# Attention and MLP-mixer on one core: the weighted sum P·V in plain float32, two heads side by side on TensorE

## The chip, the cores and the metric

One Trainium2 chip, one of its cores. The metric is the device time of one execution in microseconds (us). The kernel before took 702.86 us, the median of 3 runs (702.39 to 704.26).

## The reference

q, k and v are [4, 8, 576, 64] in float32: batch, heads, positions, head size. All matrix products are asked for in float32, and the output is float32.

```python
q_rot, k_rot = (rotate(q), rotate(k))            # rotary positions, halves of 32
scores = scale * np.matmul(q_rot, k_rot.transpose(0, 1, 3, 2))
scores = scores - np.max(scores, axis=-1, keepdims=True)
attn = np.exp(scores)
attn = attn / (np.sum(attn, axis=-1, keepdims=True) + 1e-09)
x = np.matmul(attn, v)                           # then heads side by side: [4, 576, 512]
h = np.maximum(x.transpose(0, 2, 1) @ w_tok1, 0.0) @ w_tok2        # [576, 256], [256, 576]
u = x + h.transpose(0, 2, 1)
out = u + np.maximum(u @ w_ch1, 0.0) @ w_ch2     # [512, 1536], [1536, 512]
```

The weights of the mixer come as 64-bit floats and are split on the chip.

## The kernel before

**Two stages.** `attention` (L205) works through 16 pairs of heads, `mixers` (L669) through the token and the channel products. Between them stands the splitting of the token weights (`tok_weights`, L642), which is queued into the first pairs of attention: each block of 512 columns is taken apart by `f64_split` (L579) in some ten instructions on ACT, DVE and POOL.

**Two-part numbers.** TensorE multiplies `float32r`, a float32 cut to fewer bits, in one pass. So every factor is kept as a high part (ACT writes it, rounded) and a low part (DVE subtracts the high part from the original), and a product is made of several float32r matmuls.

**A pair.** 576 positions are four blocks of 128 and a tail of 64. A pair of heads has nine tiles of scores: four blocks for each head, and one tile that holds both heads' tails (`TILES`, L394). For each tile: the scores on TensorE (`qk`, L426 and L435, 4 or 6 matmuls of 288 columns), the negated row maximum on DVE (`mx`, L440), the exponential with its row sum on ACT (`ex`, L450), four transpositions of P on TensorE (`tr`, L460), a copy of the high part by ACT (`eh`, L465) and the subtraction that makes the low part by DVE (`el`, L469). The last 64 columns of P go in groups of two or three tiles through `tt_` (L490), `th` (L496) and `tl` (L499).

**The weighted sum.** The transposed P of a head is collected in two chunks of 256 or 320 query columns. A chunk takes nine matmuls (`pv`, L514). The stationary operand is V with its high part in columns 0 to 63 and its low part in columns 64 to 127 (made by POOL, L272 and L275), so one matmul multiplies with both; four row blocks go once with the high part of P, four with its low part, and in the ninth both parts of the tail stand above each other. The sums for V's two parts come out on the two halves of the partitions, so ACT copies one half (`p1`, L517) and DVE adds the other (`p2`, L520) into `oT`. Then `oT` is transposed back (L547, L550), copied to X (L556) and divided by the row sums (L566, L559).

**The order.** No loop sets it. `Plan` (L56) is a list scheduler: each piece is a task with an engine, an estimated duration, what it depends on, the buffers that it holds and a priority; a piece with alternatives goes to the engine that would end it first. Priorities in attention are the pair's and tile's number plus an offset per kind of piece, the table `AT` (L143). `SLACK` (L145) says how much later than the earliest possible piece a piece may start and still be taken for its priority. Scores have two PSUM buffers (`s`), everything else of TensorE's results shares four (`t`).

Of the kernel before, what the change touches and what calls it, by code (L numbers as in the profile page):

```python
# [55 lines left out]
class Plan:  # L56


    def __init__(self):
        self.tasks = []  # L60
        self.clock = {e: 0.0 for e in LAG}

# [25 lines left out]
    def run(self):  # L88
# [10 lines left out]
        while left:  # L99
# [13 lines left out]
            for eng, lst in best.items():  # L113
                first = min(x[0] for x in lst)
                x = min((x for x in lst if x[0] <= first + SLACK[eng]), key=lambda x: (x[1], x[0]))
                if pick is None or x[0] < pick[0]:
                    pick = x
# [34 lines left out]
def dve(n):  # L152
    return n / 960 + 0.07
# [15 lines left out]
def rope_attention_mixer_kernel(ctx: ExitStack, tc: tile.TileContext, q, k, v, w_tok1, w_tok2, w_ch1, w_ch2, tab, out):  # L169
# [8 lines left out]
    nc = tc.nc  # L178
# [26 lines left out]
    def attention(ctx):  # L205
# [3 lines left out]
        def slots(nm, n, shape, dt=F32, pool=pers, fifo=True):  # L209
# [4 lines left out]
               "v": slots("vraw", 1, [P, 2, R + 1, D])}  # L214
# [32 lines left out]
        def prep(n):  # L247
# [4 lines left out]
            for nm, src, pr in (("k", k, 0.0), ("q", q, 0.5), ("v", v, 1.0)):  # L252
# [12 lines left out]
                if nm == "v":  # L265
                    l.append(add("SP", 0.65, ldt(TL), bufs=[rb], prio=pos + AT["load"] + pr))
                n5 = 2 * (R + 1) * D
                if nm == "v":
                    vb = Buf(vss)

                    def v1(e, rb=rb, vb=vb):
                        return lambda: e.tensor_copy(out=vb.t[:, :, :, 0:D], in_=rb.t.rearrange("p h r d -> p r h d"))  # L272

                    def v2(e, rb=rb, vb=vb):
                        return lambda: e.tensor_tensor(out=vb.t[:, :, :, D:2 * D], in0=rb.t.rearrange("p h r d -> p r h d"),  # L275
                                                       in1=vb.t[:, :, :, 0:D], op=ALU.subtract)
# [117 lines left out]
        TILES = [(0, 0), (0, 1), (0, 2), (0, 3), None, (1, 2), (1, 3), (1, 0), (1, 1)]  # L394
        CHUNK = [(0, 1), (2, 3, 4), (4, 5, 6), (7, 8)]
        W2 = S // 2

        def pair(n):
            b, hp = divmod(n, HP)
            lb = Buf(ls)  # L400
            pt = [Buf(pts) for _ in CHUNK]
            pb, tr_done, exps, el_of = {}, {}, {}, {}
# [5 lines left out]
            chunk_ev = {c: [] for c in range(4)}  # L408

            def dests(t):  # L410
                if t == 4:
                    return [(1, 0, TL, 2 * P), (2, TL, TL, 2 * P)]
                c = {0: 0, 1: 0, 2: 1, 3: 1, 5: 2, 6: 2, 7: 3, 8: 3}[t]
                return [(c, 0, P, TILES[t][1] % 2 * P)]

            oT = Buf(oTs)
            pv_done = []
            for t in range(9):
                g = 9 * n + t
                sb = Buf(s_ps)  # L420
                if TILES[t] is None:
# [6 lines left out]
                else:  # L428
                    h, j = TILES[t]
# [15 lines left out]
                def ex(sb=sb, nm=nm, p=pb[t], t=t):  # L445
                    if TILES[t] is None:
                        l = lb.t[:, R, 0:1]
                    else:
                        l = lb.t[:, TILES[t][1], TILES[t][0]:TILES[t][0] + 1]
# [3 lines left out]
                x = add("ACT", 0.73, ex, [x], [sb, nm, pb[t], lb], g + AT["ex"])  # L453
                exps[t] = x
                tb = Buf(t_ps)
                new = [pt[c] for c, s0, w, d0 in dests(t)]
# [5 lines left out]
                x = add("PE", 0.45, tr, [x], [tb, pb[t]] + new, g + AT["tr"])  # L462
                for c, s0, w, d0 in dests(t):
                    def eh(tb=tb, c=c, s0=s0, w=w, d0=d0):
                        nc.scalar.copy(out=pt[c].t[:, 0:R, d0:d0 + w],  # L465
                                       in_=tb.t.rearrange("p (j q) -> p j q", j=R)[:, :, s0:s0 + w])

                    def el(tb=tb, c=c, s0=s0, w=w, d0=d0):
# [7 lines left out]
                end = {1: 0, 4: 1, 6: 2, 8: 3}.get(t)  # L476
                if end is None:
                    continue

                ts = {0: (0, 1), 1: (2, 3, 4), 2: (5, 6), 3: (7, 8)}[end]  # L480
                tb = Buf(t_ps)
                ev = {}
                for x, tt in enumerate(ts):
                    for c, s0, w, d0 in dests(tt):
                        a = ev.setdefault(c, [x * P + s0, d0, 0])
                        a[2] += w

                def tt_(tb=tb, ts=ts):
                    for x, tt in enumerate(ts):
                        nc.tensor.transpose(tb.t[0:TL, x * P:(x + 1) * P], pb[tt].t[:, M:S], ident)  # L490

                x = add("PE", 0.11 * len(ts), tt_, [exps[tt] for tt in ts],
                        [tb] + [pb[tt] for tt in ts] + [pt[c] for c in ev], g + AT["tt"])
                for c, (s0, d0, w) in ev.items():
                    def th(tb=tb, c=c, s0=s0, w=w, d0=d0):
                        nc.scalar.copy(out=pt[c].t[0:TL, R, d0:d0 + w], in_=tb.t[0:TL, s0:s0 + w])  # L496

                    def tl(tb=tb, c=c, s0=s0, w=w, d0=d0):
                        nc.vector.tensor_tensor(out=pt[c].t[TL:P, R, d0:d0 + w], in0=tb.t[0:TL, s0:s0 + w],  # L499
                                                in1=pt[c].t[0:TL, R, d0:d0 + w], op=ALU.subtract)  # L500
                    x3 = add("ACT", act(w), th, [x], [tb, pt[c]], g + AT["th"])
                    x4 = add("DVE", dve(w), tl, [x3], [tb, pt[c]], g + AT["tl"])
                    chunk_ev[c] += [x3, x4]
# [419 lines left out]
```

## Time and profile before

The profiled execution spans 700.2 us from its first to its last instruction. The median of the runs, 702.86 us, is 2.7 us above that; this much lies around the span.

| engine | busy us | share of the span |
|---|---|---|
| PE (TensorE matmul) | 655.4 | 94% |
| PEld (its weight loads) | 589.1 | 84% |
| DVE | 513.6 | 73% |
| ACT | 378.0 | 54% |
| POOL | 332.9 | 48% |

How to read it: the shares are averages over two unlike stages. The attention stage lasts until about 328 us, the mixers from there to the end. A matmul's busy time contains its way through the array, so busy time of PE overstates what it has to do; the distance from one matmul's start to the next one's start is the better measure.

### The profile page before, as it was taken

How to read it: one execution, taken by the hardware profiler on the slowest of the kernel's cores; microseconds unless marked ns; L12 is line 12 of the kernel's file. 1: busy time of each engine (PE TensorE's matmuls, PEld its weight loads, DVE VectorE, ACT ScalarE, POOL GpSimd, SP SyncE). 2: the span in 40 equal slices, each digit the busy share in tenths (PEclk: the TensorE clock that was granted, in tenths of full speed). 3: DMA queues.
4: the chain of work that ended last, by engine and by line, in shares of the span. 5: the costliest groups of instructions: out<-in, count | busy, mean ns of one | idle time of the engine just before them, and what ended most of it. 6: DMA issues, size and time to landing. Idle time of an engine off the chain costs nothing.

```text
span 700.2 us, 11545 instructions
## 1 busy us (share of the span) xinstructions
PE 655.4 (94%) x3960; PEld 589.1 (84%) x3960; DVE 513.6 (73%) x937; ACT 378.0 (54%) x917; POOL 332.9 (48%) x348
## 2 busy tenths in 40 slices
PE   1778989999999999996999999999999999999997
PEld 1667878899999999995787998998989989899895
DVE  5999999999999999997785789736943583233322
ACT  3678888899999999996443444422421321111010
POOL 3989997887777777602650546502700250000000
PEclk9999999999999999999899999999999999999999
DMA  7466545465655555450110123201300100001112
GB/s 204 128 171 164 139 117 146 103 155 148 147 148 145 148 146 148 113 149 0 54 60 1 46 76 105 76 1 61 90 31 0 62 1 1 0 1 46 75 61 90
DMA packets 45433, 62.28 MB, mean 89 GB/s; under 512 B 13888, under 2 KB 26944, under 8 KB 45376
## 3 DMA queue, kind: packets, MB, share of 16 engines
q1 hardware_dynamic: 44832, 60.91, 32.3%
q8 instruction: 31, 0.51, 0.3%
q10 hardware_dynamic: 544, 0.66, 0.3%
q14 instruction: 26, 0.21, 0.1%
HBM read 30.41 MB, written 4.72 MB: 50 GB/s over the span
## 4 chain that ended last, share of the span: by engine, by line
PE 60%; DVE 27%; ACT 6%; issue 4%; DMA 2%; POOL 0%; DVEq 0%; SPq 0%; ACTq 0%; POOLq 0%
PE m L801 21%; PE m L824 21%; DVE nm L440 9%; DVE pt L469 8%; PE m L718 4%; PE m L740 4%; PE t L514 3%; DVE oT L520 2%; ACT p L450 2%; DVE pt L499 2%; ACT pt L465 1%; PE s L435 1%; DVE ql L335 1%; PE m L779 1%; PE t L460 1%
## 5 line engine op out<-in xcount | busy, mean ns | idle before, releaser
L803 ACT ACTIVATE gh<-m 128x384 fp32r<-128x384 f32 x72 | 35.5, 493 | 190.8 <-PE m L801 174.6
L450 ACT ACTIVATE p<-s,nm 128x576 f32<-128x576 f32 x144 | 107.9, 750 | 17.0 <-DVE nm L440 14.6
L440 DVE TENSOR_REDUCE nm<-s 128x1 f32<-128x576 f32 x144 | 107.3, 746 | 1.6 <-PE s L435 0.8
L469 DVE TENSOR_TENSOR pt<-t,pt 128x512 fp32r<-128x512 f32 (+1 forms) x160 | 97.6, 628 | 3.0 <-ACT pt L465 1.7
L801 PE MATMUL m<-uh,c1h 128*128 128x384 f32 x288 | 97.0, 337 | 0.0
L801 PE MATMUL m<-uh,c1l 128*128 128x384 f32 x288 | 96.6, 336 | 0.0
L801 PE MATMUL m<-ul,c1h 128*128 128x384 f32 x288 | 96.6, 335 | 0.0
L514 PE MATMUL t<-pt,vs 128*128 128x256 f32 (+1 forms) x576 | 92.3, 304 | 4.1 <-DVE pt L469 2.0
L805 DVE SCALAR_TENSOR_TENSOR gl<-m,gh 128x384 fp32r<-128x384 f32 x72 | 39.6, 555 | 70.5 <-ACT gh L803 70.3
L435 PE MATMUL s<-khd,qs 128*128 128x288 f32 x256 | 81.9, 336 | 8.1 <-ACT p L450 7.2
L460 PE MATMUL t<-ident,p 128*128 128x128 f32 x576 | 85.0, 275 | 4.4 <-DVE pt L499 2.7
L514 PEld LDWEIGHTS t<-pt,vs 128*128 128x128 f32 x576 | 78.8, 188 | 10.5 <-DVE pt L469 3.9
L826 DVE TENSOR_TENSOR X<-m,X 128x512 f32<-128x512 f32 x64 | 44.2, 690 | 58.6 <-PE m L824 58.6
L465 ACT CAST pt<-t 128x512 fp32r<-128x512 f32 (+1 forms) x160 | 84.1, 550 | 5.3 <-PE t L460 4.4
L824 PE MATMUL m<-c2h,gl 128*128 128x512 f32 x216 | 85.1, 394 | 0.0
L824 PE MATMUL m<-c2l,gh 128*128 128x512 f32 x216 | 85.0, 393 | 0.0
L824 PE MATMUL m<-c2h,gh 128*128 128x512 f32 x216 | 84.8, 393 | 0.0
L460 PEld LDWEIGHTS t<-ident,p 128*128 128x128 f32 x576 | 67.5, 141 | 7.6 <-DVE pt L499 3.4
L435 PE MATMUL s<-kld,qs 128*128 128x288 f32 x256 | 72.5, 299 | 0.0
L435 PEld LDWEIGHTS s<-khd,qs 128*128 128x128 f32 x256 | 49.2, 192 | 16.2 <-ACT p L450 13.2
L611 POOL TENSOR_TENSOR fa<-fc,fa 128x384 f32<-128x384 f32 (+2 forms) x24 | 28.7, 1199 | 57.2 <-DVE fa L609 57.2
L801 PEld LDWEIGHTS m<-uh,c1h 128*128 128x128 f32 x288 | 54.1, 188 | 0.9
(126 smaller groups left out, 1355.6 us busy)
## 6 DMA issues: line engine op xcount, KB each, us to landing
khd<-kh SPq DMA_DIRECT2D x62, 144.0 KB, 2.5
kld<-kl SPq DMA_DIRECT2D x62, 144.0 KB, 2.7
stg<-in_moe_w_ch_dram SPq DMA_DIRECT2D x16, 384.0 KB, 3.2
stg<-in_moe_w_ch_dram SPq DMA_DIRECT2D x12, 512.0 KB, 3.6
kraw<-in_k_dram SPq DMA_DIRECT2D x16, 256.0 KB, 3.0
qraw<-in_q_dram SPq DMA_DIRECT2D x16, 256.0 KB, 3.1
vraw<-in_v_dram SPq DMA_DIRECT2D x16, 256.0 KB, 2.9
out_dram<-X SPq DMA_DIRECT2D x16, 256.0 KB, 2.1
```

The source lines that it names most:

```text
L435: nc.tensor.matmul(sb.t[:, c, 0:W2], a, m.t[:, h, c * W2:(c + 1) * W2], start=(x == 0), stop=(x == 1))
L440: nc.vector.tensor_reduce(out=nm.t, in_=sb.t[:, :, 0:W2], axis=AX.XY, op=ALU.max, negate=True)
L450: nc.scalar.activation(out=p.t.rearrange("p (a b) -> p a b", a=2), in_=sb.t[:, :, 0:W2], func=ACTF.Exp, bias=nm.t, accum_out=l)
L460: nc.tensor.transpose(tb.t[:, j * P:(j + 1) * P], p.t[:, j * P:(j + 1) * P], ident)
L465: nc.scalar.copy(out=pt[c].t[:, 0:R, d0:d0 + w], in_=tb.t.rearrange("p (j q) -> p j q", j=R)[:, :, s0:s0 + w])
L469: nc.vector.tensor_tensor(out=pt[c].t[:, R + 1:2 * R + 1, d0:d0 + w], in0=tb.t.rearrange("p (j q) -> p j q", j=R)[:, :, s0:s0 + w], in1=pt ...
L514: nc.tensor.matmul(ab.t[:, 0:w], vb.t[:, r, h], pt[c].t[:, j, 0:w], start=(x == 0), stop=(x == 2 * R))
L801: nc.tensor.matmul(tb.t[:, 0:N], a, m, start=(i == 0), stop=(i == len(lst) - 1))
L803: x = add("ACT", 0.49, lambda f=f, tb=tb: nc.scalar.activation(out=gb.t[0][:, f], in_=tb.t[:, 0:N], func=ACTF.Relu), [x], [tb, gb], pr + f)
L805: y = add("DVE", 0.56, lambda f=f, tb=tb: nc.vector.scalar_tensor_tensor(out=gb.t[1][:, f], in0=tb.t[:, 0:N], scalar=0.0, in1=gb.t[0][:, f ...
L824: nc.tensor.matmul(tb.t, a, m, start=(i == 0), stop=(i == len(lst) - 1))
L826: y = add("DVE", 0.69, lambda u=u, tb=tb: nc.vector.tensor_tensor(out=u, in0=tb.t, in1=u, op=ALU.add), [z] + sums.get((ci, x), []), [tb], ...
```

## The change

1. V is no longer split. The weighted sum's stationary operand is the raw float32 V of one head, 64 columns wide, straight from the load buffer `vraw`, of which there are now two. POOL's two pieces per pair and the buffers `vs` and `tmp` are gone, and so is the second load of V's tail.
2. Transposed P is copied once, as float32, by ACT or DVE, whichever the planner takes (`both`). There is no low part of P any more, for the blocks as for the tails.
3. The chunks now hold both heads: two chunks per pair, of 256 and 320 query columns. A chunk takes ten plain float32 matmuls, five row blocks for each head; head 0 writes partitions 0 to 63 of the result, head 1 partitions 64 to 127, in turn. The tail's row block has only 64 rows of P; the other 64 rows of the buffer and of `vraw` are zeroed once at the start.
4. The result is copied to `oT` in one piece (`p1`); there is no addition.
5. The tiles of a pair alternate between the heads (`ORDER`), except in the first pair (`ORDER0`); the tails go in groups of four, three and two. The table `AT` and `SLACK` are new for attention; the mixers keep the old `SLACK`.

```diff
-AT = {"qk": -30.7, "mx": 30.06, "ex": -2.13, "tr": 1.27, "eh": -10.75, "el": 15.57, "tt": -24.59, "th": -29.34, "tl": -21.22, "pv": -7.19, "p1": -4.38, "p2": -3.09, "fin": 15.37, "f6": -15.84, "load": 0.72, "rot": -5.73, "pt": -7.68, "dup": -17.69, "vs": -36.1}
+AT = {"qk": -1.07, "mx": 21.16, "ex": -245.4, "tr": 3.28, "eh": 24.96, "el": 22.11, "tt": -104.81, "th": -124.9, "tl": -26.25, "pv": -61.6, "p1": 75.58, "p2": -70.34, "fin": 25.84, "f6": -173.86, "load": -15.11, "rot": 56.69, "pt": -7.0, "dup": -35.55, "vs": -7.99}
 FIRST = -60.0
-SLACK = {"PE": 0, "ACT": 0, "DVE": 0, "POOL": 0, "SP": 0.18}
+SLACK = {"PE": 0.06, "ACT": 0.06, "DVE": 0.34, "POOL": 0.05, "SP": 0.19}
...
-               "v": slots("vraw", 1, [P, 2, R + 1, D])}
+               "v": slots("vraw", 2, [P, 2, R + 1, D])}
...
-        vss = slots("vs", 2, [P, R + 1, 2, 2 * D], F32R)
         ps = slots("p", 4, [P, S])
-        pts = slots("pt", 3, [P, 2 * R + 1, 2 * P + TL], F32R)
+        pts = slots("pt", 3, [P, R + 1, 2, 2 * P + TL])
         oTs = slots("oT", 2, [P, S])
-        tmps = slots("tmp", 1, [D, 2 * P + TL])
         ls = slots("l", 3, [P, R + 1, 2])
         ris = slots("ri", 2, [P, R + 1, 2])
...
-        for nm in "qk":
+        for nm in "kqv":
...
+        for _, _, t in pts.free:
+            nc.gpsimd.memset(t[TL:P, R], 0.0)
...
-                    l.append(add("SP", 0.65, ldt(TL), bufs=[rb], prio=pos + AT["load"] + pr))
...
-                    x = add("POOL", 0.74, v1(nc.gpsimd), l + last, [rb, vb], pos + AT["vs"])
-                    x = add("POOL", 1.56, v2(nc.gpsimd), [x], [rb, vb], pos + AT["vs"])
-                    ready_v[n] = (x, vb)
+                    ready_v[n] = (l, rb)
...
-        TILES = [(0, 0), (0, 1), (0, 2), (0, 3), None, (1, 2), (1, 3), (1, 0), (1, 1)]
-        CHUNK = [(0, 1), (2, 3, 4), (4, 5, 6), (7, 8)]
+        ORDER = [(0, 0), (1, 0), (0, 1), (1, 1), None, (0, 2), (1, 2), (0, 3), (1, 3)]
+        ORDER0 = [(0, 0), (0, 1), (0, 2), (0, 3), (1, 0), (1, 1), None, (1, 2), (1, 3)]
...
+            def both(fn, n, *args, prio):
+                return add("ACT", act(n), fn(nc.scalar.copy), *args, prio, alts=[("DVE", dve(n), fn(nc.vector.tensor_copy))])
...
-                for c, s0, w, d0 in dests(t):
-                    def eh(tb=tb, c=c, s0=s0, w=w, d0=d0):
-                        nc.scalar.copy(out=pt[c].t[:, 0:R, d0:d0 + w],
-                                       in_=tb.t.rearrange("p (j q) -> p j q", j=R)[:, :, s0:s0 + w])
-                        nc.vector.tensor_tensor(out=pt[c].t[:, R + 1:2 * R + 1, d0:d0 + w],
-                                                in0=tb.t.rearrange("p (j q) -> p j q", j=R)[:, :, s0:s0 + w],
-                                                in1=pt[c].t[:, 0:R, d0:d0 + w], op=ALU.subtract)
-                    x3 = add("ACT", act(R * w), eh, [x], [tb, pt[c]], g + AT["eh"])
-                    x4 = add("DVE", dve(R * w), el, [x3], [tb, pt[c]], g + AT["el"])
-                    chunk_ev[c] += [x3, x4]
...
+                def cp(e, tb=tb, c=c, d0=d0, at=tiles[t]):
+                    def go():
+                        src = tb.t.rearrange("p (j q) -> p j q", j=R)
+                        if at is None:
+                            e(out=pt[c].t[:, 0:R, :, d0:d0 + TL], in_=src.rearrange("p j (h q) -> p j h q", h=2))
+                        else:
+                            e(out=pt[c].t[:, 0:R, at[0], d0:d0 + P], in_=src)
+                    return go
+                chunk_ev[c].append(both(cp, R * P, [x], [tb, pt[c]], prio=g + AT["eh"]))
...
+                        def tcp(e, tb=tb, z=z, k=k, dst=dst, how=how, kw=kw):
+                            return lambda: e(out=dst(), in_=tb.t[0:TL, z * P:(z + k) * P].rearrange(how, **kw))
+                        chunk_ev[c].append(both(tcp, k * P, [x], [tb, pt[c]], prio=g + AT["th"]))
...
-                def pv(c=c, h=h, w=w, ab=ab):
-                    order = list(range(R)) + list(range(R + 1, 2 * R + 1)) + [R]
-                    for x, j in enumerate(order):
-                        r = j if j <= R else j - R - 1
-                        nc.tensor.matmul(ab.t[:, 0:w], vb.t[:, r, h], pt[c].t[:, j, 0:w], start=(x == 0), stop=(x == 2 * R))
-                def p1(w=w, ab=ab, tm=tm):
-                    nc.scalar.copy(out=tm.t[:, 0:w], in_=ab.t[D:P, 0:w])
-
-                def p2(w=w, ab=ab, tm=tm, h=h, c0=c0):
-                    nc.vector.tensor_tensor(out=oT.t[h * D:(h + 1) * D, c0:c0 + w], in0=ab.t[0:D, 0:w], in1=tm.t[:, 0:w], op=ALU.add)
...
+                def pv(c=c, w=w, ab=ab):
+                    for r in range(R + 1):
+                        for h in range(2):
+                            nc.tensor.matmul(ab.t[h * D:(h + 1) * D, 0:w], vb.t[:, h, r, :], pt[c].t[:, r, h, 0:w],
+                                             start=(r == 0), stop=(r == R))
+
+                def p1(e, w=w, ab=ab, c0=c0):
+                    return lambda: e(out=oT.t[:, c0:c0 + w], in_=ab.t[:, 0:w])
+
+                x = add("PE", 5 * w * 4 * 0.00044, pv, chunk_ev[c] + vdone, [ab, vb, pt[c]], g + AT["pv"])
+                pv_done.append(both(p1, w, [x], [ab, oT], prio=g + AT["p1"]))
...
+        plan.slack = {"PE": 0, "ACT": 0, "DVE": 0, "POOL": 0, "SP": 0.18}
```

How this moves the work, at two places that the prediction speaks of. First TensorE in a middle pair, around a weighted sum. Before (t is PSUM, pt the transposed P, vs the split V, s scores, p the exponentials):

```order
L490 MATMUL t_134<-ident,p_113 64x128
L490 MATMUL t_134<-ident,p_112 64x128
L460 MATMUL t_135<-ident,p_113 128x128 x4
L460 MATMUL t_136<-ident,p_112 128x128 x4
L514 MATMUL t_133<-pt_116,vs_110 128x320 x9
L435 MATMUL s_132<-khd_103,qs_107 128x288
L435 MATMUL s_132<-kld_105,qs_107 128x288
```

The changed kernel, the same engine (vraw is the V as loaded; L498 is the new `pv`, L465 the tails, L445 the blocks, L414 and L423 the scores, L314 and L316 the next pair's k and q):

```order
L414 MATMUL s_130<-kh_99,bd_110 128x288 x2
L414 MATMUL s_130<-kl_100,bd_110 128x288
L498 MATMUL t_132<-pt_115,vraw_94 64x320 x10
L465 MATMUL t_134<-ident,p_114 64x128
L465 MATMUL t_134<-ident,p_111 64x128
L465 MATMUL t_134<-ident,p_112 64x128
L465 MATMUL t_134<-ident,p_113 64x128
L314 MATMUL t_131<-ident,uq_97 128x128 x2
L316 MATMUL t_131<-ident,uq_97 128x128
L445 MATMUL t_133<-ident,p_114 128x128 x4
L423 MATMUL s_129<-khd_104,qs_108 128x288
```

The four sums of a pair with nine full-width matmuls have become two with ten half-width ones, and tails of four tiles go together.

Second DVE in the early pairs, where the token weights are split. Before (fa, fh and fc are the splitter's buffers, w1l a token weight's low part):

```order
L469 TENSOR_TENSOR pt_118<-t_135,pt_118 128x4x128
L607 SCALAR_TENSOR_TENSOR fh_71<-stg_66,fa_69 128x512
L520 TENSOR_TENSOR oT_119<-t_136,tmp_121 64x320
L440 TENSOR_REDUCE nm_127<-s_131 128x1
L499 TENSOR_TENSOR pt_118<-t_133,pt_118 64x256
L335 TENSOR_TENSOR ql_101<-t_134,qh_100 128x256
L335 TENSOR_TENSOR ql_101<-t_135,qh_100 128x320
L469 TENSOR_TENSOR pt_118<-t_136,pt_118 128x4x128
L609 TENSOR_SCALAR fa_69<-fh_71 128x512
```

The changed kernel, DVE in the first pair:

```order
L322 TENSOR_TENSOR ql_102<-t_131,qh_101 128x320
L601 TENSOR_TENSOR w1l<-fh_70,w1h 128x512
L586 TENSOR_SCALAR fa_69<-fa_69 128x512
L518 RECIPROCAL ri_123<-l_120 128x10
L588 SCALAR_TENSOR_TENSOR fh_71<-stg_66,fa_69 128x512
L590 TENSOR_SCALAR fa_69<-fh_71 128x512
L592 TENSOR_TENSOR fa_69<-fc_73,fa_69 128x512
L594 TENSOR_TENSOR fh_71<-fh_71,fa_69 128x512
L428 TENSOR_REDUCE nm_126<-s_130 128x1
L428 TENSOR_REDUCE nm_127<-s_129 128x1
L601 TENSOR_TENSOR w1l<-fh_71,w1h 128x512
```

Before, the splitter's pieces stand one by one between attention's, spread over the first five pairs; now they stand in runs, and all within the first three pairs.

## Rows read from the trace of the kernel before

**Rows 1.** Busy time by stage: stretch and its length, PE, PEld, DVE, ACT, POOL.

```profile
0.00:17.24 17.24, 2.73 (x9) 1.56 (x10) 9.88 (x26) 6.42 (x13) 5.10 (x16) 1.00 0.71 206
17.24:158.91 141.67, 125.21 (x889) 110.82 (x888) 135.80 (x252) 117.73 (x302) 122.51 (x134) 1.00 0.56 141
158.91:301.45 142.54, 139.34 (x1072) 131.71 (x1072) 138.07 (x273) 131.23 (x345) 105.47 (x123) 1.00 0.58 145
301.45:327.90 26.45, 23.80 (x175) 21.57 (x175) 22.55 (x45) 21.14 (x55) 2.58 (x4) 1.00 0.22 66
340.00:700.20 360.20, 355.00 (x1790) 316.30 (x1788) 199.51 (x328) 96.85 (x196) 91.67 (x70) 1.00 0.14 43
```

**Rows 2.** Timeline of PE: the transpositions that close a pair, start and length.

```profile
158.91 0.66 PE L547 MATMUL t<-ident,oT 128*128 128x128 f32 x4
176.73 0.66 PE L547 MATMUL t<-ident,oT 128*128 128x128 f32 x4
```

**Rows 3.** One pair: busy PE, PEld, DVE, ACT, POOL, granted clock last but two.

```profile
158.91:176.73 17.82, 17.41 (x134) 16.45 (x134) 17.26 (x35) 16.41 (x44) 14.00 (x17) 1.00 0.58 149
```

**Rows 4.** Chain of waits over that pair, shares by line, its beginning.

```profile
by line: DVE nm L440 29.3%; DVE pt L469 23.7%; PE t L514 8.7%; issue 8.0%; DVE oT L520 7.3%; DVE pt L499 5.5%; PE t L547 3.7%; DVE ql L335 3.5%; PE s L435 3.0%; DVE kl L335 2.7%; PE t L460 2.5%; DVE ri L537 1.2%; PE t L550 0.6%; DVEq L335 0
```

**Rows 5.** That pair, DVE: lines L469, L499, L520, one row each.

```profile
158.91:176.73 17.82, 6.14 (x11) 1.00 0.58 149
158.91:176.73 17.82, 1.87 (x5) 1.00 0.58 149
158.91:176.73 17.82, 1.78 (x4) 1.00 0.58 149
```

**Rows 6.** That pair, ACT: lines L465, L496, L517, one row each.

```profile
158.91:176.73 17.82, 5.30 (x10) 1.00 0.58 149
158.91:176.73 17.82, 1.61 (x5) 1.00 0.58 149
158.91:176.73 17.82, 1.59 (x4) 1.00 0.58 149
```

**Rows 7.** Timeline of PE in a later pair: start, length, instructions.

```profile
216.10 0.38 PE L490 MATMUL t<-ident,p 128*64 128x128 f32 x2
216.32 1.03 PE L460 MATMUL t<-ident,p 128*128 128x128 f32 x8
217.20 1.58 PE L514 MATMUL t<-pt,vs 128*128 128x320 f32 x9
218.62 0.29 PE L435 MATMUL s<-khd,qs 128*128 128x288 f32 x1
218.75 0.29 PE L435 MATMUL s<-kld,qs 128*128 128x288 f32 x1
...
227.15 1.23 PE L514 MATMUL t<-pt,vs 128*128 128x256 f32 x9
228.21 0.60 PE L460 MATMUL t<-ident,p 128*128 128x128 f32 x4
```

**Rows 8.** Groups by line and shape: count, busy us, mean ns of one.

```profile
L469 DVE TENSOR_TENSOR pt<-t,pt 128x512 fp32r<-128x512 f32 x128 | 85.9, 682 | 2.5 <-ACT pt L465 1.3
L465 ACT CAST pt<-t 128x512 fp32r<-128x512 f32 x128 | 74.4, 593 | 4.9 <-PE t L460 4.3
L605 DVE TENSOR_SCALAR fa<-fa 128x512 uint32<-128x512 uint32 x16 | 10.5, 659 | 0.9 <-POOL fa L603 0.9
L613 DVE TENSOR_TENSOR fh<-fh,fa 128x512 f32<-128x512 f32 x4 | 5.0, 1247 | 0.0
```

**Rows 9.** Timeline of the start: POOL's buffer clearing and identity, PE's first work.

```profile
1.12 0.57 POOL L240 MEMSET bd<- 128x256 f32 x2
...
2.25 0.29 POOL masks.py:199 TENSOR_SCALAR_AFFINE_SELECT ident<-ident 128x128 f32<-128x128 f32 x1
...
6.43 0.66 PE L327 MATMUL t<-ident,uk 128*128 128x128 f32 x2 [6.43 <-DVE uk L298]
```

More of the change, by code (lines that the diff above doesn't have):

```diff
@@ L114, in run @@
                 first = min(x[0] for x in lst)
-                x = min((x for x in lst if x[0] <= first + SLACK[eng]), key=lambda x: (x[1], x[0]))
+                x = min((x for x in lst if x[0] <= first + self.slack[eng]), key=lambda x: (x[1], x[0]))
                 if pick is None or x[0] < pick[0]:
@@ L400, in pair @@
             lb = Buf(ls)
-            pt = [Buf(pts) for _ in CHUNK]
-            pb, tr_done, exps, el_of = {}, {}, {}, {}
+            pt = [Buf(pts) for _ in range(2)]
+            pb, exps = {}, {}
             kdone, (khd, kld) = ready_k[n]
@@ L407, in pair @@
             vdone, vb = ready_v[n]
[L408 to L414, printed above, removed]
+            chunk_ev = {0: [], 1: []}
+            tiles = ORDER if n else ORDER0
+            tails = {3: (0, 1, 2, 3), 6: (4, 5, 6), 8: (7, 8)} if n else {1: (0, 1), 3: (2, 3), 5: (4, 5), 8: (6, 7, 8)}
+            place = lambda t: (1, 2 * P) if tiles[t] is None else (tiles[t][1] // 2, tiles[t][1] % 2 * P)
+            ends = {max(t for t in range(9) if place(t)[0] == c): c for c in range(2)}
+            def both(fn, n, *args, prio):
+                return add("ACT", act(n), fn(nc.scalar.copy), *args, prio, alts=[("DVE", dve(n), fn(nc.vector.tensor_copy))])
             oT = Buf(oTs)
@@ L420, in pair @@
                 sb = Buf(s_ps)
-                if TILES[t] is None:
+                if tiles[t] is None:
                     def qk(sb=sb):
@@ L428, in pair @@
                 else:
-                    h, j = TILES[t]
+                    h, j = tiles[t]
                     def qk(sb=sb, h=h, j=j):
@@ L443, in pair, with ex @@
                 pb[t] = Buf(ps)
[L445 to L449, printed above, removed]
+                def ex(sb=sb, nm=nm, p=pb[t], at=tiles[t]):
+                    l = lb.t[:, R, 0:1] if at is None else lb.t[:, at[1], at[0]:at[0] + 1]
                     nc.scalar.activation(out=p.t.rearrange("p (a b) -> p a b", a=2), in_=sb.t[:, :, 0:W2], func=ACTF.Exp,
                                          bias=nm.t, accum_out=l)
-                x = add("ACT", 0.73, ex, [x], [sb, nm, pb[t], lb], g + AT["ex"])
+                x = add("ACT", 0.65, ex, [x], [sb, nm, pb[t], lb], g + AT["ex"])
                 exps[t] = x
                 tb = Buf(t_ps)
-                new = [pt[c] for c, s0, w, d0 in dests(t)]
+                c, d0 = place(t)
                 def tr(tb=tb, p=pb[t]):
@@ L492, in pair @@
[L492 to L503, printed above, removed]
@@ L516, in p1 @@
[L516 to L524 removed]
+                x = add("PE", 0.45, tr, [x], [tb, pb[t], pt[c]], g + AT["tr"])
@@ new lines, in pair, with tt_ @@
+                if t in tails:
+                    ts = tails[t]
+                    tb = Buf(t_ps)
+                    def tt_(tb=tb, ts=ts):
+                        for x, tt in enumerate(ts):
+                            nc.tensor.transpose(tb.t[0:TL, x * P:(x + 1) * P], pb[tt].t[:, M:S], ident)
+                    x = add("PE", 0.11 * len(ts), tt_, [exps[tt] for tt in ts],
+                            [tb] + [pb[tt] for tt in ts] + [pt[c] for c in {place(tt)[0] for tt in ts}], g + AT["tt"])
+                    runs = []
+                    for z, tt in enumerate(ts):
+                        if tiles[tt] is None:
+                            runs.append((1, z, 1, lambda c=1: pt[c].t[0:TL, R, :, 2 * P:2 * P + TL], "p (h q) -> p h q", {"h": 2}))
+                    z = len(runs)
+                    c, d0 = place(ts[z])
+                    k = len(ts) - z
+                    if n == 0:
+                        runs.append((c, z, k, lambda c=c, d0=d0, h=tiles[ts[z]][0], k=k: pt[c].t[0:TL, R, h, d0:d0 + k * P], "p q -> p q", {}))
+                    elif k == 2:
+                        runs.append((c, z, k, lambda c=c, d0=d0: pt[c].t[0:TL, R, :, d0:d0 + P], "p (h q) -> p h q", {"h": 2}))
+                    else:
+                        runs.append((c, z, k, lambda c=c, d0=d0: pt[c].t[0:TL, R, :, d0:d0 + 2 * P].rearrange("p h (j q) -> p j h q", j=2),
+                                     "p (j h q) -> p j h q", {"h": 2, "j": 2}))
+                    for c, z, k, dst, how, kw in runs:
+                        def tcp(e, tb=tb, z=z, k=k, dst=dst, how=how, kw=kw):
+                            return lambda: e(out=dst(), in_=tb.t[0:TL, z * P:(z + k) * P].rearrange(how, **kw))
+                        chunk_ev[c].append(both(tcp, k * P, [x], [tb, pt[c]], prio=g + AT["th"]))
@@ new lines, in pair @@
+                if t not in ends:
+                    continue
+                c = ends[t]
+                w = 2 * P + (TL if c == 1 else 0)
+                c0 = 2 * P * c
+                ab = Buf(a_ps)
+                def pv(c=c, w=w, ab=ab):
[3 more added lines that the diff above has]
+                                             start=(r == 0), stop=(r == R))
```

31 lines of the change are left out of this document (1 added, 30 removed).

## The prediction

> **What bounds the kernel now.** I read the busy times by stage first [rows 1]. From 340 us on PE is busy for 355 of 360 us: the mixers are TensorE's, the change leaves them alone, and I give them the same time. Attention lasts to about 328 us; there PE and DVE are both near full and the rest is not. The transpositions that close a pair recur every 17.82 us [rows 2], so one stretch of that length is a pair: DVE is busy for 17.26 of it, ACT for 16.41, POOL for 14.00, PE by the modelled ends for 17.41 [rows 3]. Who sets the pace is told by the chain of waits over this pair: the row maximum 29%, the low part of P 24%, the tails' low part 5%, the addition of the sum's two halves 7%, k's and q's low parts 6%, all on DVE; TensorE has some 18% in all [rows 4]. So DVE bounds attention, at 97%.
>
> How far behind is PE? Its busy time overstates it, so I count steps from start to start [rows 7]. A score matmul takes 0.13 us (218.62 to 218.75), a transposition 0.11 (eight from 216.32 to 217.20), a weighted sum 1.42 for 320 columns (217.20 to 218.62) and 1.06 for 256 (227.15 to 228.21). A pair has 134 matmuls: 38 of scores, 60 transpositions, 36 of sums. That is 38 x 0.13 + 60 x 0.11 + 2 x (1.42 + 1.06) = 4.9 + 6.6 + 5.0 = 16.5 us. TensorE is only 1.3 us per pair behind DVE. Whatever is taken from DVE, in the steady stretch no more than that can come back unless TensorE's own work shrinks.
>
> **DVE, ACT and POOL.** From DVE go the low parts of P and the addition: 6.14 + 1.87 + 1.78 = 9.8 us per pair [rows 5]. Back come, as the planner dealt them out, 67 of the 144 block copies, 31 of the 65 tail copies and one copy of a sum. A copy is not in the trace; the subtraction of the same shape takes 0.68 [rows 8] and I use that as the upper end, with 0.37 for a tail (1.87 / 5): 4.2 x 0.68 + 1.9 x 0.37 = 3.6 us. DVE comes to 17.3 - 9.8 + 3.6 = 11.1. ACT loses 5.30 + 1.61 + 1.59 = 8.5 [rows 6] and gets 77 block copies at 0.59 [rows 8], 34 tails at 0.32 and 31 sums at 0.40, over 16 pairs 4.4: 12.3. POOL loses V's two pieces. None of the three is late next; TensorE is.
>
> **TensorE.** Scores and transpositions keep their number: 11.5 us. The 36 float32r matmuls become 20 plain float32 ones, five row blocks for two heads over 256 + 320 columns. No row shows a plain float32 product. The nearest one is the float32 transposition, 0.11 us for 128 columns or 0.86 ns a column: with both heads side by side 5 x 576 x 0.86 = 2.5 us. The other end is four one-pass products at the float32r rate (1.06 us / 9 / 256 = 0.46 ns a column), one head after the other: 10 x 576 x 1.84 = 10.6 us. I take four passes, because the full product of two factors of two parts has four terms, at 0.44 ns between the two rates, and the halves side by side: 5 x 576 x 1.77 = 5.1 us, near the 5.0 that it replaces. TensorE then needs 16.6 us a pair.
>
> That plain float32 takes four passes is also what the Trainium skill says (FP8 and Floating Point Precision, TensorE Precision Notes). That column tiles run beside each other, it says too (TensorEngine Tiling (Array Packing), Key Properties); no run here shows either.
>
> One row speaks on the change of tile width: two transpositions with a 64-wide stationary operand, in the midst of 128-wide work, take their two steps of 0.11 (216.10 to 216.32) and nothing more [rows 7]. The same section of that page says that changing the tiling mode drains TensorE. A drained matmul costs its length less its step, 0.29 - 0.13 = 0.16 us; 32 sums with a change before and after each would add 64 x 0.16 = 10 us. By the row it is nothing; it is kept among the rivals.
>
> **The pace after.** TensorE needs 16.6 us and will not be without waits: scores still have two buffers, each held through matmul, maximum and exponential, and PE stood 1.3 us a pair before. I take 0.9 (0.2 to 1.5 in the range): 17.5 us a pair.
>
> **The sum, against the profiled 700.2 us** [rows 1].
> - 0 to 17.24: the chain to the first scores is DVE's and stays. POOL clears three more buffers of 640 columns and V's tails ahead of the identity: 0.29 per 256 columns makes some 2.4 us, so the identity is ready near 5.0 and not 2.5; its first reader starts at 6.43 [rows 9]. Nothing; without that cover 1 us.
> - 17.24 to 158.91, 141.7 us: 889 matmuls, 6.6 pairs at 17.5 are 116. Before, DVE had the token weights beside attention here. Now they stand in the first three pairs, in runs: some 27 instructions at 0.66 to 1.25 [rows 8], about 23 us on DVE. Three pairs then ask 3 x 11.1 + 23 = 56 of DVE against 52 of TensorE: 4 us. A run of six splitter steps without a maximum (5 us) starves the scores once: 5 us, less if the two sums queued on PE there cover it. The filling of the pipe: 6 us. 116 + 15 = 131, a gain of 10.6 (bounds 5 to 23).
> - 158.91 to 301.45: eight pairs, 140 for 142.5, a gain of 2.5.
> - 301.45 to 327.9: 175 matmuls, 1.3 pairs, 22.9, and the run-out of 3.2 without one handover (0.7): 25.4, a gain of 1.1.
> Together 14.2: a span of 686.0. The median of the runs stands 2.7 above the span, so 688.7, say 689. With waits of 0.2 to 1.5 us a pair and the early bounds this case reaches from 674 to 700.
>
> The added waits: the first matmul of a sum now waits for V's load itself, with all of PE queued behind it. V has two buffers and its load is issued as soon as the sum two pairs back is done, more than a pair ahead, so I give it nothing. SP has one transfer less per pair.
>
> **The rivals.**
> - *One half after the other.* The ten matmuls of a sum run in turn, 10.2 us a pair. TensorE needs 21.7, with 0.6 of waits 22.3: 16 x (22.3 - 17.5) = 77 us more, less 9 for the early crowd, which then hides: 757, slower by far. For it: in all rows matmuls start one after the other, and TensorE has 1.3 us a pair to give. Against it: no two neighbours before write different halves, so no row could show it. It decides early: the gain of 14.2 is 0.9 a pair and is gone when the sums take over 6.0 us, 59% of what they take in turn.
> - *Side by side, but with a price at each step.* A weight load that shows, at the 0.11 of a transposition, on ten row steps a pair is 1.1 us, 18 us in all: 707. The drain above gives 699. Waits of the scores at 0.8 a pair more would give 702. This is the case of no change. For it: PE's small surplus; against it: in the steady pair loads are hidden behind the matmul before.
> - *Cheaper passes.* At the transposition's rate the sums take 2.5, PE 14.0; with ACT at 12.3 the pace would be about 15: 40 us less, of which the early crowd takes back 10: 659. Only the transposition's row speaks for it.
>
> **How the numbers follow.** The forecast has 0.64, one after the other 0.17, a price at each step 0.14, cheaper passes 0.05. A measurement of this kernel can tell 0.3%, 2.1 us, from no change. Faster: 0.62 of the first, 0.05 of the third, 0.05 of the last: 0.72. Within 0.3%: 0.06. Slower: 0.17 + 0.05 = 0.22. The range of 662 to 712 holds the first case, nearly all of the third and a part of the last; the serial case is left out.
>
> **What the profile after would show.** Right: ten matmuls of 320 columns done in about 2.8 us from the first start to the next piece's start, with starts in pairs; the closing transpositions 17.5 us apart; DVE at about 11 of it; the chain of waits moved from the maximum to TensorE. Wrong on the halves: 5.6 us for such a sum and 22 us a pair. Wrong on the early pairs: the splitter's lines on the chain, and PE idle, in the first 70 us. Wrong on the bound: pairs under 17 us. The mixers should take their 360 us again.

## The result, and the profile after

The changed kernel takes 693.25 us (median of 4 runs, 691.77 to 694.02), the kernel before 703.56 beside it: a ratio of 0.9851, 95% interval 0.983 to 0.9873. Run once more, the ratio was 0.9853 (0.9837 to 0.9869). So it is 1.5% faster, about 10 us, of the 14 that were forecast; 693 lies in the range, 4 us above the predicted 689.

The busy times of the page of after, and the same stretches as in [rows 1] and the pair as in [rows 3] (stretch and length, then PE, PEld, DVE, ACT, POOL with their instructions, granted clock, DMA share, GB/s):

```profile
span 691.7 us, 11124 instructions
...
PE 660.6 (95%) x4024; PEld 557.4 (81%) x4024; DVE 429.1 (62%) x739; ACT 324.9 (47%) x755; POOL 292.7 (42%) x314
```

```profile
17.24:158.91 141.67, 133.70 (x985) 105.09 (x985) 110.64 (x182) 104.82 (x263) 107.62 (x118) 1.00 0.59 150
158.91:301.45 142.54, 141.05 (x1084) 112.82 (x1084) 94.43 (x173) 102.27 (x252) 78.41 (x100) 1.00 0.55 142
199.93:218.22 18.29, 18.09 (x141) 14.40 (x140) 11.99 (x23) 13.01 (x34) 11.72 (x15) 1.00 0.57 142
```

The reader is to see three things. DVE has fallen from 17.26 of a 17.82 us pair to 11.99 of 18.29, ACT from 16.41 to 13.01, while PE fills 18.09. The pair itself is not shorter, it is 0.47 us longer. And the early stretch holds more work: a pair is now 138 records of PE (each plain float32 matmul leaves two, so ten of them are x20 below), so 985 records are 7.1 pairs, where 889 at 134 were 6.6.

The chain of waits over that pair of after, which answers to [rows 4]:

```profile
by line: PE t L498 28.2%; PE s L423 22.9%; PE t L445 19.1%; ACT p L435 5.9%; PE s L414 5.8%; PE t L465 5.5%; DVE nm L428 4.2%; issue 4.0%; PE t L528 2.4%; PE t L314 1.2%; PE t L531 0.6%; PE t L316 0.6%; ACTq L319 0.3%; DVEq L428 0.1%
```

Over 85% of it is TensorE: the sums (L498), the scores (L423), the transpositions (L445). The row maximum, 29% before, has 4%.

The timeline of PE around the same pair of after (start, length, instruction), with both weighted sums and what follows each:

```profile
197.96 1.47 PE L445 MATMUL t<-ident,p 128*128 128x128 f32 x12
199.29 0.40 PE L423 MATMUL s<-khd,qs 128*128 128x288 f32 x1
199.52 0.30 PE L423 MATMUL s<-kld,qs 128*128 128x288 f32 x1
...
199.93 0.60 PE L528 MATMUL t<-ident,oT 128*128 128x128 f32 x4
200.36 0.49 PE L465 MATMUL t<-ident,p 128*64 128x128 f32 x3
200.78 2.38 PE L498 MATMUL t<-pt,vraw 128*64 128x256 f32 x20
203.09 0.40 PE L423 MATMUL s<-khd,qs 128*128 128x288 f32 x1
203.33 0.30 PE L423 MATMUL s<-kld,qs 128*128 128x288 f32 x1
...
210.19 0.29 PE L414 MATMUL s<-kl,bd 128*128 128x288 f32 x1
210.41 2.91 PE L498 MATMUL t<-pt,vraw 128*64 128x320 f32 x20
213.25 0.63 PE L465 MATMUL t<-ident,p 128*64 128x128 f32 x4
...
218.22 0.60 PE L528 MATMUL t<-ident,oT 128*128 128x128 f32 x4
```

The ten float32 products take 2.31 us over 256 columns (200.78 to 203.09) and 2.84 over 320 (210.41 to 213.25): 5.15 us a pair, where 5.1 was forecast. Behind the sum the first score matmul is 0.24 long from start to start (203.09 to 203.33), where behind a sum of before it was 0.13 [rows 7]. That alone is no sign of the half width: behind full-width transpositions the first one takes 0.23 as well (199.29 to 199.52; in the trace of before 171.26 to 171.49). L528 recurs after 18.29 us.

So where did 10 us come from? The two traces differ by 8.5 us, 700.2 and 691.7. Six of the 41 runs of before that were timed beside the experiments had, like the profiled one, a mean granted clock of 0.993 to 0.995, and a median of 702.2 us; the other 35 had 0.984 to 0.991 and 703.7. The eight runs of after had 0.994 to 0.998. So some 1.5 us of the ten go with more time at the lower of the clock's two levels in most runs of before; where it fell there, no trace shows. The 8.5 us can be followed. The start of the last matmul of each pair's sums, read off the timelines of PE:

| pair | before | after | earlier by |
|---|---|---|---|
| 1 | 45.2 | 39.1 | 6.1 |
| 2 | 72.0 | 64.0 | 8.0 |
| 4 | 110.3 | 103.3 | 7.0 |
| 6 | 150.0 | 139.7 | 10.3 |
| 7 | 167.9 | 158.0 | 9.9 |
| 15 | 310.5 | 302.9 | 7.6 |
| 16 | 325.7 | 317.4 | 8.3 |

All of it is there by the sixth pair, 6 us by the first; the steady pairs give back 2.3 (9.9 at pair 7, 7.6 at pair 15). The mixers take what they took: from the last closing transposition to the end of the span 372.8 us before and 373.0 after.

### The profile page after: what moved, and what is told of

Same layout as the page of the kernel before. It is cut to its first block, busy times and chain, and to the rows that moved or that the text cites. A ratio compares the mean times of both kernels' runs of the same rounds, so it can differ in the third digit from the quotient of the medians.

```text
span 691.7 us, 11124 instructions
## 1 busy us (share of the span) xinstructions
PE 660.6 (95%) x4024; PEld 557.4 (81%) x4024; DVE 429.1 (62%) x739; ACT 324.9 (47%) x755; POOL 292.7 (42%) x314
## 4 chain that ended last, share of the span: by engine, by line
PE 81%; ACT 6%; DVE 5%; issue 4%; DMA 2%; SPq 0%; POOL 0%; ACTq 0%; DVEq 0%; POOLq 0%
PE m L783 22%; PE m L806 22%; PE t L498 10%; PE s L423 7%; PE t L445 6%; PE m L700 4%; PE m L722 4%; ACT p L435 3%; DVE nm L428 2%; ACT pt L455 2%; PE s L414 2%; PE t L465 2%; PE m L761 1%; PE t L528 1%; PE t L314 1%
## 5 line engine op out<-in xcount | busy, mean ns | idle before, releaser
L423 PE MATMUL s<-khd,qs 128*128 128x288 f32 x256 | 83.2, 341 | 5.1 <-ACT p L435 4.2
L498 PE MATMUL t<-pt,vraw 128*64 128x256 f32 (+1 forms) x640 | 85.6, 411 | 0.2 <-ACT pt L455 0.2
L445 PE MATMUL t<-ident,p 128*128 128x128 f32 x576 | 77.5, 275 | 0.7 <-DVE XT L540 0.4
L423 PE MATMUL s<-kld,qs 128*128 128x288 f32 x256 | 72.7, 300 | 0.0
L498 PEld LDWEIGHTS t<-pt,vraw 128*64 128x64 f32 x640 | 44.0, 137 | 31.3 <-issue 5.1
L445 PEld LDWEIGHTS t<-ident,p 128*128 128x128 f32 x576 | 66.7, 141 | 2.1 <-DVE XT L540 0.9
L423 PEld LDWEIGHTS s<-khd,qs 128*128 128x128 f32 x256 | 49.3, 192 | 20.6 <-ACT p L435 12.8
L783 PEld LDWEIGHTS m<-ul,c1h 128*128 128x128 f32 x288 | 54.2, 188 | 0.9
L783 PEld LDWEIGHTS m<-uh,c1l 128*128 128x128 f32 x288 | 54.2, 188 | 0.0
L592 POOL TENSOR_TENSOR fa<-fc,fa 128x384 f32<-128x384 f32 (+1 forms) x23 | 27.7, 1207 | 57.7 <-DVE fa L590 57.7
```

The source lines that it names most:

```text
L423: nc.tensor.matmul(sb.t[:, c, 0:W2], a, m.t[:, h, c * W2:(c + 1) * W2], start=(x == 0), stop=(x == 1))
L445: nc.tensor.transpose(tb.t[:, j * P:(j + 1) * P], p.t[:, j * P:(j + 1) * P], ident)
L498: nc.tensor.matmul(ab.t[h * D:(h + 1) * D, 0:w], vb.t[:, h, r, :], pt[c].t[:, r, h, 0:w], start=(r == 0), stop=(r == R))
L592: mul_ = lambda e: lambda: e.tensor_tensor(out=A(), in0=C(), in1=A(), op=ALU.mult)
L783: nc.tensor.matmul(tb.t[:, 0:N], a, m, start=(i == 0), stop=(i == len(lst) - 1))
```

## The experiments

The runs of the first group ask what the sums cost TensorE; those of the second, what bounded the kernel before and where the early gain comes from. Diffs are against after unless another is named. Ratios are to the kernel before, timed beside each.

**One half after the other.**

```diff
-for r in range(R + 1):
-    for h in range(2):
+for h in range(2):
+    for r in range(R + 1):
         nc.tensor.matmul(ab.t[h * D:(h + 1) * D, 0:w], ...)
```

> The ten matmuls of a sum in another order: five of head 0, then five of head 1. Theory (the halves run beside each other only where neighbours in the queue write different halves): each sum takes twice as long, 9.4 us a pair where it was 4.7, some 4.7 us a pair and 70 to 75 us in all: about 765, pairs 22.5 to 23 us apart, matmul starts about 0.2 us apart and no two together. Rival (TensorE finds the other half's matmul in its queue whatever the order): no change, 693.

One run took 737.98 us: neither number. The timeline of PE shows the two sums of one of its pairs:

```profile
202.83 3.73 PE L498 MATMUL t<-pt,vraw 128*64 128x256 f32 x20
213.80 4.58 PE L498 MATMUL t<-pt,vraw 128*64 128x320 f32 x20
```

They take about 3.6 and 4.45 us to the next piece's start, 8.0 a pair for 5.15: 16 x 2.85 = 46 us, and the time is 45 above after's. By the starts of the single records, head 1's first four fall among head 0's last four, and from there on it is alone. So the halves run side by side when their matmuls stand next to each other in the queue, TensorE found the other half's work only some four records ahead, and the alternating order is what makes the change pay.

**A full-width matmul amid each sum, and behind it.** A float32r matmul of zeros by zeros, 128 columns wide, is added to all 32 sums, in the midst of the halves or behind them.

```diff
             for h in range(2):
                 nc.tensor.matmul(ab.t[h * D:(h + 1) * D, 0:w], ...)
+            if r == 2:    # the second kernel: behind the loop over r
+                nc.tensor.matmul(ab.t[:, 0:P], identr, identr, start=False, stop=False)
```

> One full-width float32r matmul of zeros, 128 columns, between the third and fourth row block of every sum (32 in all; it adds zeros). Theory (TensorE empties at each change between half-width and full-width work, 0.35 us for there and back): the matmul itself 2 to 4 us in all, and 32 more changes there and back, 11 us: 706 to 708, and 11 above the kernel that has the same matmul at the sum's end. Rival (what is lost at the edges of a sum is the wait for its operands, and a change of width costs nothing): 695 to 697, the same as with the matmul at the end.

> The same full-width matmul of zeros, but behind the tenth matmul of every sum, where full-width work follows anyway. Both theories: only the matmul itself, 0.06 to 0.11 us each, 2 to 4 us in all: 695 to 697.

Amid the sum: 704.62 us, ratio 1.0018 (1.0009 to 1.0027). Behind it: 695.96, 0.9895 (0.9877 to 0.9913). The added work is the same, only the 32 ways out of the halves and back differ: 8.7 us, 0.27 us each. The timeline of PE in the first of the two:

```profile
205.49 1.52 PE L500 MATMUL t<-pt,vraw 128*64 128x256 f32 x12
206.94 0.33 PE L503 MATMUL t<-identr 128*128 128x128 f32 x1
207.20 1.08 PE L500 MATMUL t<-pt,vraw 128*64 128x256 f32 x8
208.21 0.40 PE L425 MATMUL s<-khd,qs 128*128 128x288 f32 x1
```

The wide matmul holds PE for 0.26 us, 206.94 to 207.20. So the way between a sum on the halves and full-width work does cost TensorE, 0.27 us there and back. The Trainium skill says that changing the tiling mode drains TensorE (TensorEngine Tiling (Array Packing), Key Properties); the trace agrees as far as it goes. But the added matmul differs from the sum's in more than its width: it is float32r and leaves one record, where a plain float32 matmul leaves two. The neighbour's format is not what counts: the last step in front of a sum is 0.09 us longer than usual behind float32r scores (0.22 from 210.19 to 210.41, for 0.13) as behind the float32 transpositions of L465 (three steps in 0.42 from 200.36, for 0.33). Whether the half width or the sum's two records make the price is not shown: no plain float32 product at full width was run.

**Both sums of a pair back to back.** One task issues both sums, so a pair goes to the halves once.

```diff
-pts = slots("pt", 3, ...)
+pts = slots("pt", 4, ...)
...
-x = add("PE", ..., pv, chunk_ev[c] + vdone, [ab, vb, pt[c]], ...)
+x = add("PE", ..., pv, chunk_ev[0] + chunk_ev[1] + vdone, abs_ + [vb] + pt, ...)
```

> Both column sums of a pair stand back to back in TensorE's queue, so a pair enters and leaves the halves once instead of twice: 16 fewer changes there and back. Theory (the changes of width cost TensorE 0.27 us each there and back, by the difference of the two runs with wide transpositions amid and behind the sums, up to 0.35 by the timeline): 4.3 to 5.6 us less, 688 to 689 us. Rival (a block of 5 us of sums in one piece keeps new scores from VectorE and ScalarE, and the next pair waits for them): 693 to 700 us.

It took 698.31 us, 0.9929 (0.9916 to 0.9941), after beside it 693.32: the rival's time. But the steady pairs did get shorter, as this timeline of its PE shows:

```profile
209.34 0.60 PE L532 MATMUL t<-ident,oT 128*128 128x128 f32 x4
...
218.67 5.07 PE L501 MATMUL t<-pt,vraw 128*64 128x256 f32 x40
223.67 0.40 PE L424 MATMUL s<-khd,qs 128*128 128x288 f32 x1
...
227.03 0.60 PE L532 MATMUL t<-ident,oT 128*128 128x128 f32 x4
```

17.69 us a pair for 18.29. Of these 0.6 the block of sums itself explains 0.15 (5.00 us to the next start for 5.15); the rest is its edges and the other order around it, which I did not separate. What it lost, it lost early: its seventh pair's last sum matmul starts 10 us later than after's (167.9 for 158.0), and its fourth pair's already 11 (114.6 for 103.3), after the pairs that have the token weights beside them.

**Back to back in the middle only.** From that follows a version: merged in the sixth to the fifteenth of the 16 pairs (5 to 14, counted from 0 in the expectation), separate in the first five and in the last.

```diff
+if not 5 <= n < 15:
+    ...    # one sum at a time, as in after
```

> Both sums of a pair back to back as before, but only in pairs 5 to 14; the early pairs and the last keep two sums. Theory (back to back gives 0.5 us a pair in the steady stretch, 17.7 for 18.2, as the run with all sums merged showed, and what that run lost, it lost in its first seven pairs): 10 x 0.5 less, some of it back at the two changes of pattern: 688 to 691 us. Rival (the changes of pattern take it all): 692 to 697 us.

690.39 us, 0.9807 (0.9793 to 0.9821), where after had 0.9837 to 0.9869: the intervals do not touch, and of the kernels that compute the whole result this is the fastest of the study. Its steady pairs are 17.7 us apart; two of 20.1 and 19.3 us (from last sum to last sum) at the change of pattern take back part of it.

**The kernel before without the low parts of P.** If DVE set the pace at 97%, this should bring what the change brought. Against the kernel before:

```diff
-x4 = add("DVE", dve(R * w), el, [x3], ...)
-chunk_ev[c] += [x3, x4]
+chunk_ev[c] += [x3]
```

> The kernel before, with the low parts of P left at zero and never worked out (that part of the computation is left out): VectorE loses the subtractions at L469, L499 and L520, and the sums stay as they were, float32r at full width, with no change of width. Theory (VectorE set the pace before, and its relief alone brings the gain; TensorE is the bound behind it): about 17.5 us a pair or a little less and no width changes, 685 to 692 us. Rival (the gain comes from the new queue order or from the sums themselves, not from VectorE's relief): 699 us or more.

(The addition at L520 stayed; the expectation names it by mistake.) 701.75 us, 0.9973 (0.996 to 0.9986). With before's order, the theory falls. By stage:

```profile
17.24:158.91 141.67, 125.61 (x899) 116.05 (x899) 103.35 (x165) 116.78 (x306) 118.20 (x125) 0.96 0.56 143
158.91:301.45 142.54, 137.38 (x1058) 128.31 (x1056) 80.68 (x152) 128.59 (x339) 103.32 (x122) 1.00 0.54 140
```

DVE went from 138 to 81 us of the steady 142.5, and no more matmuls fitted in (1058 for 1072): pairs are 17.9 us apart on average, where before had 17.8 (singly they range from 16.0 to 22.1, so its order has become uneven). The chain of waits of this kernel says who stands in DVE's place, first from 17.24 to 100 us, then from 100 to 158.9, then over the steady pairs:

```profile
by line: issue 9.7%; POOL w L294 9.6%; PE t L514 8.5%; PE t L462 7.9%; PE s L437 6.0%; POOL uk L296 5.8%; DVE nm L442 5.1%; POOL bd L390 4.6%; POOL uq L296 4.6%; POOL vs L277 3.9%; POOL uk L298 3.6%; DVE fh L607 2.6%; DVE fa L609 2.6%; PE s
```

```profile
by line: ACT p L452 23.1%; ACT pt L467 17.0%; issue 10.3%; DMA qs<-ql 8.3%; DVE nm L442 6.5%; PE s L437 6.5%; ACT tmp L517 4.7%; ACT pt L497 4.4%; PE t L462 4.1%; PE t L514 4.1%; ACT kh L334 2.5%; DVE kl L337 2.1%; ACT qh L334 2.0%; DVE oT 
```

```profile
by line: PE s L437 17.3%; PE t L514 17.2%; PE t L462 16.5%; ACT p L452 8.3%; ACT pt L467 6.0%; issue 4.7%; DMA qs<-ql 4.2%; PE t L491 3.8%; ACT tmp L517 3.6%; PE s L428 3.5%; DVE nm L442 2.8%; PE t L329 2.6%; DVE oT L520 2.0%; ACT pt L497 1
```

Early it is POOL, with the rotation of k and q and V's pieces; then ACT, with the exponential and the copies of P; and in the steady pairs TensorE, with over 60%, ahead of ACT. So there the prediction's view holds that TensorE stands right behind DVE; but not even the 1.3 us of its allowance came back. (Its clock was 0.96 in the early stretch, so a few us of that stretch may be the clock's.)

**... and without the sums' low matmuls too.** Against the last kernel:

```diff
-order = list(range(R)) + list(range(R + 1, 2 * R + 1)) + [R]
+order = list(range(R + 1))
```

> The kernel before without the low parts of P and without the four matmuls of each sum that read them (both left out of the computation): against the run without the low parts alone (701.75 us, pairs 17.9 us apart, ScalarE 128.6 of 142.5 us busy in the steady stretch) TensorE loses 16 matmuls a pair, 2.2 us, and ScalarE nothing. Theory (with VectorE relieved, ScalarE at 90% with its chain of exponential, copy of P and copy of a half is as near as TensorE, so the pace falls by less than half of the 2.2): pairs 17.0 to 17.9 us apart, 686 to 701 us. Rival (TensorE alone held that run): pairs about 15.8 us apart, 33 us less in all, 666 to 674 us.

687.24 us, 0.9766 (0.9751 to 0.978): the theory's range. 2.2 us of TensorE's work gone per pair shortened the steady pair from 17.9 to 17.3 only, and ACT is then at 94%:

```profile
158.91:301.45 142.54, 131.97 (x973) 117.21 (x972) 83.23 (x155) 134.15 (x354) 101.74 (x120) 1.00 0.58 147
```

So before the change DVE, TensorE with its handovers and ACT stood at nearly the same length, and POOL with them early on; all this in an order that was made for other operations.

**V's split back on POOL.** After keeps all it has, and POOL works out V's rounding and remainder again, 2.3 us a pair, into a buffer that no product reads; the sums wait for it.

```diff
+x = add("POOL", 0.74, v1, l, [rb, vs], ...)
+x = add("POOL", 1.56, v2, [x], [rb, vs], ...)
-ready_v[n] = (l, rb)
+ready_v[n] = ([x], rb)
```

> The changed kernel with V's rounding and remainder worked out on GpSimd again as before, 0.7 and 1.6 us a pair, into a buffer that no product reads; the sums wait for it. Theory (GpSimd held the early pairs too: it was 74 of 83 us busy from 17 to 100 us before, and the run without low parts had GpSimd's rotary work and V's pieces on its early chain, so V's split leaving GpSimd is part of the early gain): early pairs 3 to 6 us later, 695 to 699 us. Rival (GpSimd has the room, and only VectorE's and ScalarE's relief counts): 692 to 694.5 us.

695.86 us, 0.9887 (0.9871 to 0.9903). That is 2.5 us of the ten, at the low end of what was expected. From 17.24 to 100 us, before, after and this kernel, in that order, each from its own trace:

```profile
17.24:100.00 82.76, 69.45 (x478) 60.65 (x478) 79.56 (x141) 65.44 (x168) 74.39 (x80) 1.00 0.55 140
```

```profile
17.24:100.00 82.76, 75.36 (x541) 59.51 (x541) 72.81 (x112) 63.45 (x161) 69.01 (x73) 1.00 0.60 154
```

```profile
17.24:100.00 82.76, 72.78 (x526) 56.76 (x527) 75.84 (x112) 61.79 (x154) 77.04 (x79) 1.00 0.62 156
```

POOL (the fifth busy time) goes from 69 back to 77 us, and PE gets 15 records less done in the stretch; the sixth pair's last sum matmul starts 3.2 us later than after's.

**After's operations in before's order.** The due times and slacks of the kernel before, the operations of after.

```diff
-AT = {"qk": -1.07, "mx": 21.16, "ex": -245.4, ...}
+AT = {"qk": -30.7, "mx": 30.06, "ex": -2.13, ...}
```

> The changed kernel's operations, queued by the due times and slacks of the kernel before. Theory (the gain stands on the operations and on an order that fits them alike: after's sums cost TensorE as much as before's and add the changes of width, so without its own order the 9 us of the early pairs are not reached): 700 to 712 us. Rival (the operations alone bring the gain, the order little): 692 to 696 us.

715.53 us, 1.0165 (1.0143 to 1.0188): slower than before, and beyond what the theory said. Its pairs are 16.1 and 21.9 us apart in turn, and the last sum matmul of its first pair starts at 43.9 us, where after has 39.1 and before 45.2. The same operations thus range over 22 us by their order alone. That also limits the two runs without low parts: they kept before's due times, and what they would do with due times of their own was not tried.

**The token weights spread out.** Their loads are tied to later pairs' exponentials.

```diff
-src.bitcast(U32)), [], [sb], prio)
+src.bitcast(U32)), [after[0]], [sb], prio)
```

> The loads and work of the token-weight blocks are spread over pairs 2, 4, 7, 9 and 11 instead of standing early. Theory (the crowd of early work on VectorE and ScalarE still makes TensorE idle 1 to 2 us in each 10 between 30 and 80 us, 3 to 6 us in all that can be had back): 688 to 690 us. Rival (the early loss is the filling of the pipe and the first loads, not the crowd): 692 to 695 us.

704.25 us, 1.0009 (0.9999 to 1.0019), 11 us above after and outside both expectations. Its second and third pair were 3.4 and 3.5 us earlier than after's (60.6 and 81.8 us for 64.0 and 85.3), so the crowd did cost the early pairs what the theory said. But by the sixth this was given back (139.7 for 139.7), and single pairs of 19.7, 25.1 and 20.8 us came where the weights now stood. Moving the crowd cost more than it gave back.

**DVE's subtractions put back into after.** They write to a scratch buffer, and the sums wait for them.

```diff
+chunk_ev[c].append(x3)
...
+chunk_ev[c].append(add("DVE", dve(R * P), el, [x3], [tb, pt[c]], g + AT["el"]))    # el: to a scratch buffer
```

> TensorE as changed, but DVE subtracts again after each copy of transposed P (144 of 512 columns, 65 of the tails), into a buffer that nobody reads: about 144 x 0.61 + 65 x 0.37 = 112 us of DVE, 7 a pair. Theory (the gain is DVE's relief, above all where the token weights crowd it): DVE asks 19 us a pair, above TensorE's 18.2, and the first pairs are as slow as before: 710 to 720, nothing left of the gain. Rival (the gain comes from the new order or from the shorter way of a sum's result): 693 to 698.

755.1 us, 1.073 (1.0708 to 1.0753), far beyond both. It is no clean test: DVE is busy for only 109 of the steady 142.5 us, the chain of waits there has the sums at 19% and the added subtraction at 17%, so its work alone does not explain the time; the added wait and its place in the queue are the likely rest, not separated here.

**The changed kernel again**, as the measure for three of the runs above: 693.32 us.

> The changed kernel once more, unedited, as the measure for the other three on this chip: 692 to 694.5 us for every theory.

## Why the prediction came out as it did

- *The sums on TensorE.* Right: 5.15 us a pair for 5.1, halves side by side. The split was off both ways: ten steps of 0.216 and ten of 0.270 make 4.86, less than taken, and the edges of the sums, taken as nothing, make up the rest.
- *The change of width.* Wrong, and this is the step that failed: "By the row it is nothing." The row showed transpositions of 64 columns amid full-width work [rows 7], which still take one step of 0.11; plain float32 sums on both halves pay 0.27 us there and back. Twice a pair, 16 pairs: 8.6 us, near the 10 that stood among the rivals.
- *The pace.* 17.5 was forecast, 18.25 came. Counted by steps, the matmuls of a steady pair of after add up to 16.3 us; some 0.7 is lost at the edges of the sums (0.3 of it inside the 5.15) and 1.2 in waits, most of them for scores' buffers, where 0.9 was allowed in all. So the steady pairs lost 2.3 us and did not gain 2.5.
- *The early gain.* The size was right, 10.3 us by the sixth pair for 10.6, but by luck: at the 18.25 us that a pair takes, 6.6 pairs are 121 us and not 116, so the crowd and the filling took some 10 us where 15 were put, and the two errors cancel. The reason was only part of it. It was put down to DVE's crowd; the runs show that DVE's relief alone, in before's order, brings 1.6 us in all, that POOL's relief from V's pieces is worth 2.5, and that with before's due times nothing is gained at all (1.65% slower).
- *"DVE bounds attention, at 97%."* Half right. The chain of waits before named DVE, and the busy shares with it; but ACT at 92% and TensorE at 16.5 us and its 1.3 of handovers stood at nearly the same length, and with DVE relieved the steady chain was TensorE's. The prediction saw TensorE there and capped the gain by it, which kept its number near; it also counted ACT's relief (12.3 us, measured 13.0), but not that DVE's without ACT's would bring almost nothing.
- *The rivals.* One half after the other would have been slower, as said, but at 738 and not 757, since a few matmuls overlap at the seam. The price at each step is partly what happened. Cheaper passes did not come.
- *The 2.7 around the span.* It set the median of three runs against the span of one profiled run, one of the shorter. In the 41 runs of before each stands 2.0 us above its own span, in after's 1.8.
- *Added waits.* V's load in front of the sums was given nothing. In the steady pair above it is not on the chain; from 17.24 to 100 us the chain of after has it with 3.3%, 2.7 us, which the early gain had to carry.

What stays open: how the 6 us of the first pair divide between the new order, POOL and the tile order of that pair, since each of the runs changes more than one of them; and whether the half width or the plain float32 product makes the price at the edges of a sum.

## What to carry to other kernels

When the chain of waits names one engine and two others are above 90% in the same pair, removing the named one's work alone may buy almost nothing (here 1.6 us of 703, with the order left as it was): work out the next two lengths before pricing the relief, and look at each stage by itself, since the next in line was another engine early than in the steady pairs. A sum on the halves of TensorE's columns must alternate its halves matmul by matmul, and each visit to the halves had a price here, so gather the sums where nothing waits for the block. Operations and the order they are queued in are one change; with an order made for other operations the same work can lose more than it wins.

## What the runs showed of the hardware

- A plain float32 matmul leaves two records, and over 256 columns, with the other half beside them, the records of one half follow each other every 0.216 us (0.270 over 320). That is 0.42 ns a column and pass if a product has four, below the float32r rate of [rows 7] (0.46); with the edges the ten products take the 2.31 us above.
- The two halves' records start 6 to 7 ns apart. Queued half by half, only four records of each half overlap at the seam.
- The way from a plain float32 sum on the halves to a full-width float32r matmul and back costs 0.27 us (8.7 us over 32). That the width alone does it is not shown.
- A transposition with a 64-wide stationary operand amid full-width work shows no such cost: before's two in [rows 7] take 0.22, 0.11 each, and after's four at 213.25 take 0.46 to the next start. Next to a sum it stands like full-width work: the sum's edges are there too.
